# Six output buffers instead of three, no warm matmuls and a new order of sums and scores in the first batch, in an attention plus maxout kernel

## The chip, the cores and the metric

The kernel runs on 1 core of one Trainium2 chip. The metric is the device time of one execution in microseconds (us), the median of several executions. Comparisons are made with the kernel before, timed in the same rounds on the same chip. Ratios use executions in the fast state alone and come with a 95% interval; only one execution on record was counted as slow (354.37 us, of the run with two buffers, over 1.5% above the fastest of that kernel).

Engines: PE is the matmul array, PEld its weight loads, DVE the vector engine, ACT the scalar engine, POOL the general engine that here also issues most loads, SP the engine that issues stores and transposing transfers. A transfer "lands" when all its data has arrived; the landing time is counted from its issue.

## The reference, cut to what matters

```python
# q, k, v: (8, 12, 448, 64); w1, w2, w3, w_out: (768, 768), all float32
scores = scale * np.matmul(q, k.transpose(0, 1, 3, 2))
e = np.exp(scores - m)                       # m is the row maximum
attn = e / (np.sum(e, axis=-1, keepdims=True) + np.exp(-m) + 1e-09)
x = np.matmul(attn, v)                       # then (batch * seq, 768)
h = np.maximum(np.maximum(x @ w1, x @ w2), x @ w3)
out = h @ w_out                              # (3584, 768)
```

## The kernel before

The program is written by hand in the order in which each engine executes it; the tools only add the waits. Heads are taken in groups of 4, so a batch has three groups. For a group, `scores` makes products of k and q in a PSUM buffer and ACT takes the exponential of it; `av` makes the sums over v, and DVE normalises them (`rb`, a reciprocal, `xn`). `x_transpose_pe` brings `xn` into the layout for the second part of the work, `up_piece` makes h (`p_i`), `out_piece` the result (`op_ps`, `o_sb`).

The first batch is cut into an odd part "O" and an even part "E" of the queries, so that PE can begin before all loads are in. "s" in a step is scores, ("v", g, pr) is the sum of group g, head pair pr, part "O".

```python
    out_pool = ctx.enter_context(tc.tile_pool(name="outp", bufs=3))
    ps_s = ctx.enter_context(tc.tile_pool(name="ps_s", bufs=3, space=bass.MemoryType.PSUM))
    ps_b = ctx.enter_context(tc.tile_pool(name="ps_b", bufs=2, space=bass.MemoryType.PSUM))
    # ... cut ...
    def out_piece(bp, t, c, w, queues):
        if c == 0:
            outs[0] = out_pool.tile([128, DM], FP32, tag="o_sb", name="o_sb")
        # ... cut: 6 matmuls into op_ps, DVE copies op_ps to o_sb, two stores on SP ...

    def add_out(b):            # output tiles of a batch: 3, 4, 3, 4, ...
        for t in range(0, 3) if b % 2 == 0 else range(3, 7):
            # ... two pieces of 384 columns each ...

    # ... cut; the first batch, where the change is: ...
    attend("O", 2, S01, S23, S46)
    x_transpose_pe(0, "O")
    warm(2)                    # two matmuls on zeros, result unused
    attend("O", 2, ("v", 1, 0), ("v", 1, 1), ("v", 2, 0))
    attend("E", 0, S01)
    x_transpose_pe(1, "O")
    attend("E", 0, ("v", 2, 1), S23)
    x_transpose_pe(2, "O")
    add_up(0, NE, NO, [(i, f) for i in range(2) for f in (0, 2, 4)])
    fill(STEP)                 # first p_i piece
    attend("E", 0, S46)
    # ... cut; a little later: ...
    load_v(4)
    load_qk(5)
    load_weight(3)             # the output weight, issued by POOL
    # ... cut; later still, POOL copies half blocks of q: shift_q(4, nc.gpsimd)
```

Scores and sums take turns in the three `ps_s` buffers: each waits until ACT or DVE has emptied the one of three tiles ago.

The softmax here doesn't subtract the row's maximum and nothing guards it: scores larger than these inputs give would overflow.

## Time and profile before

| | before |
|---|---|
| time, median of 4 executions | 341.54 us (341.29 to 341.90) |
| time of the execution that was profiled | 342.59 us, span 340.8 us |
| PE / DVE / ACT / POOL busy | 97% / 55% / 44% / 43% |
| share of PE in the chain of waits | 93% |

(The span runs from the first to the last instruction and is about 1.75 us shorter than the time.)

The page of the profile of before, its busy times and the head of its chain:

```profile
PE 330.3 (97%) x4174; PEld 199.6 (59%) x4174; DVE 188.4 (55%) x410; ACT 151.2 (44%) x181; POOL 146.7 (43%) x260
...
PE 93%; ACT 2%; DVE 2%; issue 1%; ACTq 0%
```

PE bounds the kernel; the only thing to win is time in which PE stands still, or work on PE that need not be done. The timeline of PE of before, where the order will change (start, duration, engine, line, operation, out<-in, count; in brackets how long the engine was idle before, and what ended it):

```profile
16.03 1.03 PE L300 MATMUL stp<-QT,KT 64*64 64x192 f16 x24 [0.27 <-DVE QT L186]
17.37 0.28 PE L300 MATMUL stp<-QT,KT 64*64 64x192 f16 x4 [0.30 <-ACT e L320]
17.57 0.40 PE L400 MATMUL xtp<-ident,xn 128*128 128x128 f16 x4
17.81 0.59 PE L171 MATMUL warm<-wz 128*128 128x512 f16 x2
18.33 0.26 PE L340 MATMUL avp<-vt,e 64*64 64x65 f16 x8
...
22.02 0.28 PE L400 MATMUL xtp<-ident,xn 128*128 128x128 f16 x2
22.68 0.28 PE L400 MATMUL xtp<-ident,xn 128*128 128x128 f16 x2 [0.37 <-DVE xn L373]
22.80 1.43 PE L440 MATMUL p_i<-xT,w 128*128 128x192 f16 x12
24.16 0.52 PE L300 MATMUL stp<-QT,KT 64*64 64x256 f16 x12
24.62 1.16 PE L440 MATMUL p_i<-xT,w 128*128 128x192 f16 x12
```

Three things are seen: the warm matmuls at 17.81, a wait for the normalised sum at 22.68, and 12 `p_i` matmuls that take 1.43 us where the next 12 take 1.16, so that a further 0.27 us of waiting (for the copy of the transpose) hides in them. From 67 us on there is one single wait of PE, in the second batch. The timeline of PE there, then of DVE, then the landing times of the two stores issued at 110.0 and 110.5 us:

```profile
114.39 3.09 PE L464 MATMUL op_ps<-w,hT 128*128 128x384 f16 x18
...
118.04 0.93 PE L357 MATMUL avp<-vx,e 128*128 128x65 f16 x24
119.72 3.56 PE L440 MATMUL p_i<-xT,w 128*128 128x448 f16 x18 [0.76 <-DVE o_sb L471]
```

```profile
115.63 0.55 DVE L471 TENSOR_SCALAR o_sb<-op_ps 128x384 f32<-128x384 f32 x1
119.11 1.02 DVE L471 TENSOR_SCALAR o_sb<-op_ps 128x384 f32<-128x384 f32 x2 [2.92 <-PE avp L357]
```

```profile
DMA to landing us min/median/max: 8.1/8.2/8.2
```

The matmuls of the fourth output tile of this batch were done by 117.5 us, but DVE copied them at 119.11. With three buffers that tile reuses the buffer of the first, whose stores landed only 8 us after their issue, the later one at 118.6 us. The wait was for a store.

### The profile page before, as it was taken

What the parts mean: (1) busy time and instruction counts of PE and PEld (TensorE: products, weight loads), DVE (VectorE), ACT (ScalarE), POOL (GpSimd) and SP (SyncE); (2) the same over time, 40 slices, a digit from 0 to 9 for tenths busy, and PEclk for the clock granted to TensorE, in tenths of its full rate; (3) what the DMA queues carried; (4) which work ended last, traced back from release to release, by engine and by line L of the source; (5) the groups of instructions that cost most, each with busy time, mean ns of one, the idle gap of its engine ahead of it and who ended that gap; (6) DMA issues with size and microseconds to landing.
All of it is one profiled execution on the core that took longest, in us unless ns stands there. A gap on an engine that the chain in (4) does not pass through costs nothing.

```text
span 340.8 us, 9819 instructions
## 1 busy us (share of the span) xinstructions
PE 330.3 (97%) x4174; PEld 199.6 (59%) x4174; DVE 188.4 (55%) x410; ACT 151.2 (44%) x181; POOL 146.7 (43%) x260
## 2 busy tenths in 40 slices
PE   7899999999999999999999999999999999999994
PEld 4668787855555645555655655565545655565552
DVE  4556675565545365546456556556556556465552
ACT  3858855654554535463544454463544454200000
POOL 8596578971937072925267070946252000000000
PEclk9999999999999999999999999999999999999999
DMA  8999999699996999999986999999960440133006
GB/s 145 190 191 206 203 205 197 115 170 212 134 164 60 178 213 110 156 138 185 157 119 90 190 199 116 155 127 194 167 115 10 119 123 3 31 78 95 0 19 167
DMA packets 84813, 46.42 MB, mean 136 GB/s; under 512 B 53281, under 2 KB 81313, under 8 KB 84769
## 3 DMA queue, kind: packets, MB, share of 16 engines
q0 software_dynamic: 29120, 21.80, 48.6%
q1 hardware_dynamic: 55264, 23.60, 36.7%
q8 instruction: 32, 0.52, 0.6%
q10 hardware_dynamic: 384, 0.39, 0.4%
q14 instruction: 13, 0.10, 0.1%
HBM read 44.04 MB, written 11.01 MB: 162 GB/s over the span
## 4 chain that ended last, share of the span: by engine, by line
PE 93%; ACT 2%; DVE 2%; issue 1%; ACTq 0%
PE p_i L440 48%; PE op_ps L464 16%; PE avp L357 12%; PE stp L300 12%; PE avp L340 2%; ACT e L320 2%; PE warm L171 1%; PE trT L225 1%; ACT QT L184 1%; DVE QT L186 1%; PE trT L209 1%; DVE xn L373 1%; PE xtp L413 0%; PE xtp L400 0%; DVE xT L406 0%
## 5 line engine op out<-in xcount | busy, mean ns | idle before, releaser
L320 ACT ACTIVATE e<-stp 128x896 f16<-128x896 f32 (+4 forms) x171 | 144.3, 905 | 138.2 <-PE stp L300 138.0
L440 PE MATMUL p_i<-xT,w 128*128 128x448 f16 (+2 forms) x972 | 173.4, 332 | 1.1 <-DVE o_sb L471 0.8
L440 PEld LDWEIGHTS <-w 128*128 128x128 f16 x972 | 90.0, 98 | 69.0 <-issue 6.6
L245 POOL COPY QT<-QT 64x384 f16<-64x384 f16 (+1 forms) x84 | 46.9, 559 | 95.4 <-DMA QT<-ld_q 65.0
L451 DVE TENSOR_TENSOR hT<-hT,p_i 128x448 f16<-128x448 f16 (+2 forms) x96 | 59.7, 621 | 43.0 <-PE p_i L440 42.8
L464 PE MATMUL op_ps<-w,hT 128*128 128x384 f16 (+2 forms) x342 | 58.1, 323 | 0.0
L300 PE MATMUL stp<-QT,KT 64*64 64x448 f16 (+2 forms) x756 | 48.4, 339 | 2.3 <-ACT e L320 0.9
L464 PEld LDWEIGHTS <-hT 128*128 128x128 f16 x342 | 32.1, 98 | 23.0 <-issue 2.0
L471 DVE TENSOR_SCALAR o_sb<-op_ps 128x384 f32<-128x384 f32 (+2 forms) x57 | 31.2, 549 | 25.8 <-PE op_ps L464 22.7
L357 PE MATMUL avp<-vx,e 128*128 128x65 f16 x1152 | 45.4, 193 | 0.0
L449 DVE CAST hT<-p_i 128x448 f16<-128x448 f32 (+2 forms) x48 | 30.0, 625 | 24.3 <-PE p_i L440 24.2
L357 PEld LDWEIGHTS <-e 128*128 128x128 f16 x1152 | 38.8, 97 | 2.3
L373 DVE TENSOR_TENSOR xn<-avp,rb 128x512 f16<-128x512 f32 (+1 forms) x54 | 34.1, 632 | 1.9
L300 PEld LDWEIGHTS <-KT 64*64 64x64 f16 x756 | 16.0, 105 | 27.0 <-issue 24.2
L367 DVE TENSOR_SCALAR rb<-avp 128x8 f32<-128x8 f32 (+1 forms) x54 | 8.9, 165 | 39.4 <-PE avp L357 39.2
L383 POOL COPY vx<-ld_v 128x768 f16<-128x768 f16 x21 | 17.2, 820 | 8.3 <-issue 4.7
L340 PEld LDWEIGHTS <-e 64*64 64x64 f16 x768 | 14.7, 107 | 8.0 <-issue 1.2
L102 POOL DMA_DIRECT2D ld_q<-in_q_dram x24 | 17.2, 718 | 2.1 <-DMA w<-in_moe_w_dram 1.1
L102 POOL DMA_DIRECT2D ld_k<-in_k_dram x24 | 17.2, 718 | 1.9 <-DMA w<-in_moe_w_out_dram 1.0
L115 POOL DMA_DIRECT2D ld_v<-in_v_dram x24 | 15.1, 631 | 2.6 <-DMA w<-in_moe_w_dram 1.4
L340 PE MATMUL avp<-vt,e 64*64 64x65 f16 x768 | 15.4, 192 | 0.5 <-ACT e L320 0.4
L112 POOL DMA_DIRECT2D ld_v<-in_v_dram x24 | 15.2, 633 | 1.2 <-DMA w<-in_moe_w_dram 1.2
(43 smaller groups left out, 88.2 us busy)
## 6 DMA issues: line engine op xcount, KB each, us to landing
out_dram<-o_sb SPq DMA_DIRECT2D x54, 192.0 KB, 3.2
ld_v<-in_v_dram POOLq DMA_DIRECT2D x48, 128.0 KB, 4.8
ld_k<-in_k_dram POOLq DMA_DIRECT2D x23, 224.0 KB, 6.2
ld_q<-in_q_dram POOLq DMA_DIRECT2D x23, 224.0 KB, 7.0
w<-in_moe_w_dram POOLq DMA_DIRECT2D x9, 384.0 KB, 9.5
w<-in_moe_w_out_dram POOLq DMA_DIRECT2D x3, 384.0 KB, 8.5
xT<-xn SPq DMA_TRANSPOSE x18, 4.3
QT<-ld_q SPq DMA_TRANSPOSE x17, 5.1
```

Source lines behind the costliest of these rows:

```text
L102: nc.gpsimd.dma_start(out=tiles[nm][:, 1 : NP * T + 1].rearrange("x (r t) d -> x r (t d)", r=NP)[:, p0:p1], in_=src[:, p0:p1],)
L245: eng.tensor_copy(out=t[d0 : d0 + HP, o * 128 : (o + n) * 128], in_=t[s0 : s0 + HP, a * 128 : (a + n) * 128],)
L300: nc.tensor.matmul(out=stp[half * HP : half * HP + HP, par, j * qn : (j + 1) * qn], lhsT=k_block(i, pr, h2, x[half]), rhs=q_cols(i, pr, h2 ...
L320: nc.scalar.activation(out=dst, in_=src, func=AF.Exp, scale=scale)
L340: nc.tensor.matmul(out=ps[half * HP : half * HP + HP, hh, j * D1 : (j + 1) * D1], lhsT=eF[hh * HP : hh * HP + HP, o : o + HP], rhs=vt[hh * ...
L357: nc.tensor.matmul(out=ps[:, hh, j * D1 : (j + 1) * D1], lhsT=eF[:, o : o + 128], rhs=vx[:, 2 * pr + hh, (x[0]), 0:D1], start=False, stop= ...
L373: nc.vector.tensor_tensor(out=xn[i][:, pr, ws[0] : ws[0] + nw].rearrange("p j h d -> p h j d"), in0=acc[:, :, :, 0:D], in1=rb[:, :, 0:nw]. ...
L440: nc.tensor.matmul(out=p_i[:, j * qn : (j + 1) * qn], lhsT=w_sb[i][:, dc, ts(fc, 128)], rhs=xT[b][:, dc, q0 : q0 + qn], start=(dc == 0), s ...
L449: nc.vector.tensor_copy(out=dst, in_=src)
L451: nc.vector.tensor_tensor(out=dst, in0=dst, in1=src, op=ALU.max)
L464: nc.tensor.matmul(out=op_ps[:, 0:w], lhsT=hT[bp][:, fc, ts(t, 128)], rhs=wout_sb[:, fc, c : c + w], start=(fc == 0), stop=(fc == NFC - 1),)
L471: nc.vector.tensor_scalar(out=o_sb[:, c : c + w], in0=op_ps[:, 0:w], scalar1=1.0 / LAMBDA, scalar2=None, op0=ALU.mult,)
```

## The change

The intent: no output tile waits for an old store; the two sums of group 2 stand next to each other, with the first scores of part E moved ahead of them, so that DVE gets the last normalisation earlier; the warm matmuls go.

```diff
-    out_pool = ctx.enter_context(tc.tile_pool(name="outp", bufs=3))
+    out_pool = ctx.enter_context(tc.tile_pool(name="outp", bufs=6))
 # ... cut ...
     x_transpose_pe(0, "O")
-    warm(2)
-    attend("O", 2, ("v", 1, 0), ("v", 1, 1), ("v", 2, 0))
+    attend("O", 2, ("v", 1, 0))
     attend("E", 0, S01)
+    attend("O", 2, ("v", 1, 1), ("v", 2, 0), ("v", 2, 1))
     x_transpose_pe(1, "O")
-    attend("E", 0, ("v", 2, 1), S23)
+    attend("E", 0, S23)
     x_transpose_pe(2, "O")
```

## The prediction

> **What bounds the kernel.** TensorE. The page of the profile shows PE busy 330.3 of 340.8 us (97%), clock 1.0; the chain of waits is 93% PE; DVE (55%), ACT (44%) and POOL (43%) mostly wait for PE. Only idle time of PE can be won. (The Trainium skill, "Trainium Kernel Development and Optimization", Best Practices, distrusts matmul busy time as a measure; I use it only to find idle spots, which the timeline confirms.)
>
> **What the change does.** Order differs in one place on PE and DVE; ACT, POOL and SP keep theirs.
>
> 1. *Six output buffers.* In the timeline from 67 us on PE stands still in one place: at 119.72 us p_i waits 0.76 us for DVE's o_sb. DVE had been idle 2.92 us before that copy (the releaser named, an avp matmul, was long done: it was something else). It is the fourth output tile of batch 1, so with three buffers it reuses the first, whose stores were issued at 110.0 and 110.5 us and took 8.2 and 8.1 us to land (median of all stores 3.2): until about 118.6; copy at 119.11. Loads of k and q beside it took 9 us too; that all issuers share the same DMA engines, as the skill says ("DMA: Bandwidth & Descriptors", Issuing engines are not separate DMA queues), fits. With six buffers the copy runs at about 117 us and PE saves 0.76 us. Elsewhere, the last stage included, copies follow PE at 0.42 us: nothing to win.
>
> 2. *Reordering, 17.6 to 24.2 us.* The two warm matmuls (17.81, 0.43 us of issue) go. The sum behind them needs a buffer whose exp ends at 18.02; with 0.06 us from exp to PE it starts at about 18.1 instead of 18.33: 0.2 us won, the rest of the warm time becomes a wait. The E scores behind it need the next exp (ends 18.72), just met. Today the chain then runs rb 0.17, reciprocal 0.19, xn 0.44, transposes 0.30, xT copy 0.37, with PE waiting 0.37 us for xn at 22.68 and about 0.3 us for xT, p_i resuming at 23.41. With the second sum of group 2 ahead of group 1's transpose, DVE's four normalisations (about 0.85 us each) stand nearly back to back and set the pace: last xn done at about 22.17 instead of 22.63, p_i resumes at about 22.96. Gain 0.45 us in all, warm share included. The third chunk of the first weight (issued 12.3, 9.9 us to landing) is in by then, barely.
>
> Later waits are relative to PE; the second weight (in at about 30.7, used at 31.7) leaves 0.5 us, so the gain should survive.
>
> **Predicted time.** 341.7 - 0.76 - 0.45 = 340.5; I say 340.6, since the slow landing may be shorter in unprofiled runs. Range 339.7 to 341.5. Faster by over 2%: 0.5%; within 2%: 99%; slower: 0.5%.
>
> **What would show it.** Right: no PE wait near 118 us, o_sb there about 0.4 us behind its matmul; p_i resuming near 23.0; the scores now at 24.16 at 23.7; then a constant shift of 0.45, later 1.2 us. Wrong, part 1: another wait takes its place (earlier stores colliding with the transposing transfers). Wrong, part 2: first sum still at 18.3, or p_i held by the weight load.
>
> **What would make it wrong.** A store wait that is rarer or larger without the profiler; buffers released later than I computed, so that the second sums wait for ACT; gains given back to ACT waits between 24 and 41 us.

## The result, and the profile after

| | before | after |
|---|---|---|
| time, median of 4 executions each | 341.54 us (341.29 to 341.90) | 341.12 us (340.78 to 341.43) |
| ratio | | 0.9987, interval 0.9969 to 1.0004 |
| profiled execution, time | 342.59 us | 341.03 us |
| profiled execution, span | 340.8 us | 339.3 us |

A ratio is the mean time of one kernel's runs over that of the other's of the same rounds, so not quite the ratio of the medians quoted. The interval here includes 1: the timed runs alone do not show the gain, and the argument below rests on traces. (The prediction starts from 341.7 us because only three of the four executions of before had been timed then.)

The profiles differ by 1.5 us, the medians by 0.42 us. The two numbers cannot both be the worth of the change. The page of after shows the same kind of kernel:

```profile
PE 329.4 (97%) x4172; PEld 198.9 (59%) x4172; DVE 189.3 (56%) x410; ACT 151.1 (45%) x181; POOL 146.6 (43%) x260
...
PE 91%; ACT 2%; DVE 2%; DMA 2%; issue 1%; POOL 1%; POOLq 0%; ACTq 0%
```

The timeline of PE of after, at the place of the new order:

```profile
15.94 1.03 PE L300 MATMUL stp<-QT,KT 64*64 64x192 f16 x24 [0.27 <-DVE QT L186]
17.27 0.28 PE L300 MATMUL stp<-QT,KT 64*64 64x192 f16 x4 [0.30 <-ACT e L320]
17.48 0.40 PE L400 MATMUL xtp<-ident,xn 128*128 128x128 f16 x4
17.97 0.26 PE L340 MATMUL avp<-vt,e 64*64 64x65 f16 x8
...
21.64 0.29 PE L400 MATMUL xtp<-ident,xn 128*128 128x128 f16 x2
22.21 0.28 PE L400 MATMUL xtp<-ident,xn 128*128 128x128 f16 x2 [0.28 <-DVE xn L373]
22.47 1.29 PE L440 MATMUL p_i<-xT,w 128*128 128x192 f16 x12
23.69 0.52 PE L300 MATMUL stp<-QT,KT 64*64 64x256 f16 x12
24.14 1.16 PE L440 MATMUL p_i<-xT,w 128*128 128x192 f16 x12
```

The first sum follows the transpose sooner, the wait for `xn` fell from 0.37 to 0.28 us, and the `p_i` matmuls take 1.29 instead of 1.43 us. The timeline of PE of after in the second batch, then of DVE:

```profile
113.92 3.09 PE L464 MATMUL op_ps<-w,hT 128*128 128x384 f16 x18
...
118.33 3.56 PE L440 MATMUL p_i<-xT,w 128*128 128x448 f16 x18
```

```profile
115.16 0.55 DVE L471 TENSOR_SCALAR o_sb<-op_ps 128x384 f32<-128x384 f32 x1
116.06 0.56 DVE L471 TENSOR_SCALAR o_sb<-op_ps 128x384 f32<-128x384 f32 x1 [0.36 <-PE op_ps L464]
117.04 0.56 DVE L471 TENSOR_SCALAR o_sb<-op_ps 128x384 f32<-128x384 f32 x1 [0.42 <-PE op_ps L464]
```

The copies follow their matmuls, and PE does not wait: the wait of 0.76 us is gone.

**How the traces are compared from here on.** The start of the program is not the same from one execution to the next: the first scores of group 2 (the 24 matmuls at 16.03 above) start anywhere from 15.55 to 16.22 us in the profiles, in an order of instructions that is the same up to there. One source is at the very start. The Trainium skill ("TensorE: Matmul & The Clock Gate", What's actually happening) says that the number of slow first matmuls varies from run to run. It does here: the seven transposes at 4.9 us took 0.94 us in before and 0.57 in e1. Another source was a wait of 0.36 us for a load of q at 9.93 us in e1. So I measure from these scores on: to the second `p_i` piece (24.62 above), and to the `p_i` after the fourth output tile (119.72 above). For the kernels with three or more output buffers that differ in nothing but the parts of the change, that gives (us):

| kernel | output buffers | order | warm | to 2nd p_i | to p_i of second batch | span |
|---|---|---|---|---|---|---|
| before | 3 | old | yes | 8.59 | 103.69 | 340.8 |
| before, again | 3 | old | yes | 8.59 | 102.76 | 339.8 |
| buffers alone | 6 | old | yes | 8.58 | 102.76 | 339.7 |
| no warm | 3 | old | no | 8.35 | 102.53 | 341.5 |
| no warm, 6 buffers | 6 | old | no | 8.35 | 102.53 | 339.5 |
| new order, warm kept | 3 | new | yes | 8.41 | 102.59 | 339.2 |
| order alone | 3 | new | no | 8.20 | 102.38 | 339.2 |
| after | 6 | new | no | 8.20 | 102.39 | 339.3 |
| after, again | 6 | new | no | 8.21 | 102.39 | 339.2 |
| new order, 4 buffers | 4 | new | no | 8.21 | 102.38 | 339.6 |

Kernels with the same order and the same warm matmuls agree within 0.01 us over 100 us, with one exception: the first profile of before, 0.93 us longer than all others of its kind.

### The profile page after: what moved, and what is told of

It is laid out like the page before. It is cut to its first block, busy times and chain, and to the rows that moved or that the text cites. A ratio compares the mean times of both kernels' runs of the same rounds, so it can differ in the third digit from the quotient of the medians.

```text
span 339.3 us, 9812 instructions
## 1 busy us (share of the span) xinstructions
PE 329.4 (97%) x4172; PEld 198.9 (59%) x4172; DVE 189.3 (56%) x410; ACT 151.1 (45%) x181; POOL 146.6 (43%) x260
## 4 chain that ended last, share of the span: by engine, by line
PE 91%; ACT 2%; DVE 2%; DMA 2%; issue 1%; POOL 1%; POOLq 0%; ACTq 0%
PE p_i L440 48%; PE op_ps L464 16%; PE avp L357 11%; PE stp L300 11%; PE avp L340 2%; ACT e L320 2%; DMA ld_q<-in_q_dram 2%; DVE xn L373 1%; PE trT L225 1%; DVE QT L186 1%; PE xtp L413 0%; ACT QT L184 0%; POOL ld_k L102 0%; PE xtp L400 0%; DVE rb L370 0%
## 5 line engine op out<-in xcount | busy, mean ns | idle before, releaser
L471 DVE TENSOR_SCALAR o_sb<-op_ps 128x384 f32<-128x384 f32 (+2 forms) x57 | 31.3, 549 | 23.7 <-PE op_ps L464 23.5
L449 DVE CAST hT<-p_i 128x448 f16<-128x448 f32 (+2 forms) x48 | 30.0, 625 | 23.7 <-PE p_i L440 23.6
```

The source lines that it names most:

```text
L449: nc.vector.tensor_copy(out=dst, in_=src)
L471: nc.vector.tensor_scalar(out=o_sb[:, c : c + w], in0=op_ps[:, 0:w], scalar1=1.0 / LAMBDA, scalar2=None, op0=ALU.mult,)
```

## The experiments

Theory A: the wait for the store is typical of the kernel before; the buffers are worth 0.76 us. Theory B: the profiled execution of before was an untypical one; the buffers are worth nothing in most executions, and what the medians show is the order alone.

### e1_before_again: the kernel before, once more

Edit: none.

> The kernel before, unchanged, profiled and timed a second time. Theory A (the store wait is typical of it): the span is again about 340.8 us and the 0.76 us wait of the p_i matmuls near 119.7 us is there again. Theory B (the profiled execution of before, 342.59 us against a median of 341.5, was an untypical one and the store wait is rare or smaller otherwise): span about 339.8 us, wait near 119.7 us absent or under 0.3 us. Ratio to before 1.000 in both; its interval is the noise of this method.

Measured: median 341.55 us, ratio to before 0.9992 (0.9976 to 1.0009), span 339.8 us. DVE and PE at the place of the wait, and the landing times of the same two stores:

```profile
115.70 0.55 DVE L471 TENSOR_SCALAR o_sb<-op_ps 128x384 f32<-128x384 f32 x1
117.50 1.02 DVE L471 TENSOR_SCALAR o_sb<-op_ps 128x384 f32<-128x384 f32 x2 [1.25 <-DMA out_dram<-o_sb]
```

```profile
118.10 0.93 PE L357 MATMUL avp<-vx,e 128*128 128x65 f16 x24
118.87 3.57 PE L440 MATMUL p_i<-xT,w 128*128 128x448 f16 x18
```

```profile
DMA to landing us min/median/max: 6.0/6.2/6.5
```

DVE waits for the store here too, and this time the profile names it. But the store took 6.5 us at most instead of 8.2, DVE copied at 117.50, and PE had not run out of its two `ps_b` buffers. DVE waits at this copy in all five profiles with three buffers (1.21 to 2.92 us); PE feels it only when the landing is late enough. From the first profile: the copy started at 119.11 and cost 0.93 us, so a copy by about 118.2, or a landing within about 7.2 us, would have cost nothing (an estimate from these numbers, with the 0.48 us that passed between the landing at 118.63 and the copy). The second profile is as theory B expected: span 339.8 us, no wait of PE.

### e2_buffers_alone: six buffers, old order

```diff
-name="outp", bufs=3
+name="outp", bufs=6
```

> Six output buffers, old order. Theory A: 0.7 to 0.8 us faster than before (ratio 0.9978), no PE wait near 119 us. Theory B: no more than 0.2 us faster (ratio 0.9994 or more), since the wait it removes is mostly not there.

Measured: median 341.77 us, ratio 1.0001 (0.9982 to 1.0020). In the trace the way to the second batch is 102.76 us, exactly as in before again. The timed runs show no gain of the buffers alone. Their interval still allows about 0.6 us either way, but the 0.76 us of theory A (ratio 0.9978) lies just outside it. One of the six executions took 342.82 us with six buffers, where a store would have to take some 20 us to be waited for (an estimate from the pauses given in e13), so late stores are very likely not the only cause of slow executions; that execution was not profiled.

### e3_order_alone: new order, three buffers

```diff
 (the change, with bufs=3)
```

> New order, three output buffers. Both theories expect the scores after the first p_i piece about 0.4 us earlier (23.7 instead of 24.2). Theory A: 0.4 us faster than before, and the store wait of 0.7 us is still there near 119 us. Theory B: 0.4 us faster, as fast as the whole change, store wait absent or different from profile to profile.

Measured: median 341.25 us against 341.68, ratio 0.9982 (0.9965 to 0.9999). In the trace 8.20 and 102.38 us, the same as the whole change, and no PE wait in the second batch (DVE waited 1.34 us before the copy at 117.04, which fits the store of the first tile that landed about 116.5; that is within the slack). In these traces the order and the missing warm matmuls are the whole gain when no store is late.

### e4_no_warm: only the warm matmuls taken out

```diff
     x_transpose_pe(0, "O")
-    warm(2)
     attend("O", 2, ("v", 1, 0), ("v", 1, 1), ("v", 2, 0))
```

> Old order and three buffers, only the two warm matmuls taken out. The first sum of group 1 starts at about 18.1 instead of 18.3 us; if the chain of DVE normalisations passes this on, 0.2 us faster in the trace at 24 us (scores at 23.95). If the warm matmuls are needed to keep the array's clock up, the matmuls after 18 us become longer and the time does not fall.

Measured: in the trace 8.35 instead of 8.59 us, so 0.24 us of the 0.43 us in which PE issues the two warm matmuls is won, and kept to the second batch (102.53). The matmuls that follow do not become longer. But the time was no better, median 341.80 us, from 340.78 to 343.63, with two of six executions over 343 us. The profiled one (343.23 us) shows why, in PE and DVE of the fourth batch:

```profile
194.87 0.93 PE L357 MATMUL avp<-vx,e 128*128 128x65 f16 x24
197.66 1.67 PE L440 MATMUL p_i<-xT,w 128*128 128x448 f16 x8 [1.86 <-DVE o_sb L471]
```

```profile
192.47 0.55 DVE L471 TENSOR_SCALAR o_sb<-op_ps 128x384 f32<-128x384 f32 x1
197.05 1.02 DVE L471 TENSOR_SCALAR o_sb<-op_ps 128x384 f32<-128x384 f32 x2 [4.03 <-DMA out_dram<-o_sb]
```

The same wait, at another fourth tile, now worth 1.86 us: the slower of the first tile's two stores took 8.8 us to land. So two of the five profiles with three buffers show a stall of PE by a store (before 0.76, this one 1.86 us), and none of the eight with four or six.

### e5_order_with_warm: new order, warm matmuls kept, three buffers

```diff
 (the change, with bufs=3, and)
     x_transpose_pe(0, "O")
+    warm(2)
     attend("O", 2, ("v", 1, 0))
```

> New order with the two warm matmuls kept, three buffers: the order without the warm matmuls gone. If the start of the first sum carries through (the chain is one of PE), the scores after the first p_i piece stand about 0.2 us later than in the new order alone (23.9 against 23.69), so the order alone is worth 0.1 to 0.2 us of the 0.4. If DVE's normalisations set the pace whatever the start, it is as fast as the new order alone.

Measured: median 341.26 us, ratio 0.9990 (0.9978 to 1.0002). In the trace 8.41 us, 0.21 more than the new order alone: the first of the two expectations. With e4 the two parts can be told apart: the warm matmuls are worth 0.24 us in the old order and 0.21 in the new, the order 0.18 with them and 0.15 without; together 0.39 at the second `p_i` piece and 0.37 in the second batch.

### e6_2buf: two output buffers, to force the wait

```diff
-name="outp", bufs=3
+name="outp", bufs=2
```

> The kernel before with two output buffers, to make the wait for a store happen in every execution. Three buffers wait only when the store of three tiles ago takes over about 8 us (slack of about 2 us between the DVE wait and PE standing still); with two, the third tile of each half has about 2 to 4 us less. Expected: several PE waits released by o_sb at the halves that start near 108, 150, 187, 227, 265 us, 1 to 5 us each, and 6 to 16 us slower. If the wait near 119 us of the first profile had nothing to do with the stores, it is no slower than 1 us.

Measured: median 352.27 us over all four executions, 351.96 over the three fast ones; ratio of the fast ones 1.0276 (1.0236 to 1.0316), about 10 us slower. The waits in its profile (who waited for whom, us in total, times, longest), and one of them in the timeline of PE:

```profile
DVE o_sb L471 <- DMA out_dram<-o_sb: 16.0, 6, 5.3
...
PE op_ps L464 <- DVE o_sb L471: 6.7, 5, 3.1
...
PE p_i L440 <- DVE o_sb L471: 2.3, 3, 1.0
```

```profile
117.57 1.14 PE L464 MATMUL op_ps<-w,hT 128*128 128x384 f16 x6 [2.43 <-DVE o_sb L471]
```

PE waits 9.0 us in eight places, all through DVE, which waits for stores. This shows the mechanism by experiment, and that three buffers stood just at the edge: two cost about 10 us, three stalled PE in two of five profiles.

### e9_no_warm_6buf: no warm matmuls, six buffers

```diff
 (e4, and)
-name="outp", bufs=3
+name="outp", bufs=6
```

> Old order without the warm matmuls, six buffers. The same kernel with three buffers had two of six executions over 343 us and a 1.86 us wait for a store in its profile. If those slow executions were store waits: none over 342.2 us here and a median of about 341.4 us. If they came from anything else, such as a colder array, slow executions stay.

Measured: median 341.26 us (341.14 to 341.58), ratio 0.9992 (0.9979 to 1.0005), none of five executions over 341.6 us; the trace again 102.53 us, with no wait of PE for a store. As expected if the slow executions of e4 were late stores. Only one of those two was profiled, and these ran on another chip, so for the other this is likely and not shown.

### e13_order_4buf: new order, four buffers

```diff
 (the change, with bufs=4)
```

> New order with four output buffers. A half has at most four tiles, so four should do what six do: DVE's o_sb copies of the fourth tile near 117 and 195 us follow their matmuls by 0.42 us and do not wait for a store (with three buffers they did, by about 0.9 us or more). Same time as the whole change within 0.2 us.

Measured: median 341.32 us, ratio 0.9989 (0.9976 to 1.0001). (A half is the run of three or four output tiles that `add_out` puts in one place.) The copies of the fourth tiles start 0.36 us after DVE fell idle, released by their matmuls, at 116.10 and 193.28 us, as with six buffers; with three they started at 117.04 and 194.16 in the profile of the order alone. In this trace four are enough, because a half has at most four tiles and the halves are at least 20 us apart (the copies of one end at 308 us in before, those of the next begin at 328.9).

### e8_split_scores: part of the next scores ahead of the second transpose

PE still waits 0.28 us for `xn` at 22.21 in after. This fills the gap with work that is ready.

```diff
 (the change, and)
-    attend("E", 0, S23)
+    attend("E", 0, S23, S46[:2])
     x_transpose_pe(2, "O")
     add_up(0, NE, NO, [(i, f) for i in range(2) for f in (0, 2, 4)])
     fill(STEP)
-    attend("E", 0, S46)
+    attend("E", 0, ("s", (6,)))
```

> The changed kernel with the first two score units of the next step moved ahead of the second transpose, into the 0.28 us in which PE waits for xn at 22.2 us. Expected about 0.3 us earlier from 24 us on than the changed kernel, 0.3 us faster (340.8 us against 341.1), if ACT is not made late by it.

Measured: median 341.77 us (340.96 to 342.95), ratio 1.0005 (0.9989 to 1.0021). The expectation failed. To the second `p_i` piece it is 7.99 us, 0.21 less than after; to the second batch 103.08, 0.69 more. PE and POOL of this run show where it was lost:

```profile
39.80 3.02 PE L440 MATMUL p_i<-xT,w 128*128 128x256 f16 x24
42.99 0.38 PE L300 MATMUL stp<-QT,KT 64*64 64x448 f16 x2 [0.18 <-POOL QT L245]
43.66 0.57 PE L300 MATMUL stp<-QT,KT 64*64 64x448 f16 x6 [0.29 <-POOL QT L245]
```

```profile
39.73 1.41 POOL L126 DMA_DIRECT2D w<-in_moe_w_out_dram  x2 [1.19 <-DMA w<-in_moe_w_dram]
...
42.44 2.52 POOL L245 COPY QT<-QT 64x384 f16<-64x384 f16 x4
```

The scores of group 4 need copies of QT that POOL makes. Their input was ready at 37.6 us, but POOL first issues the three loads of the output weight (and two of v), and stood idle 1.07 and 1.19 us before two of them, for an earlier weight load to land as the profile puts it. In after the copies started at 40.92 us, in this run at 42.44, while PE came early. Much of that is chance: counted from the first scores, the copies start 24.4 to 26.0 us later in the other profiles with these issues in front of them, and 26.9 in this one. So they were at least 0.9 us later than in any other, more than the 0.2 us by which PE was early.

### e10_split_wout_late and e11_wout_late: the output weight's loads behind those copies

```diff
 (e8 for e10, the change for e11, and)
     load_v(4)
     load_qk(5)
-    load_weight(3)
 # ... cut ...
             shift_q(i + 1, nc.gpsimd)
         if first:
+            load_weight(3)
             load_qk(i + 3)
```

> The split of the scores (the run that won 0.2 us at 24 us and lost it at 43 us to POOL's copies of QT) with the loads of the output weight issued after those copies instead of before. If the loss was POOL standing behind its own weight-load issues, the QT copies start near 38.5 us instead of 42.4, no PE wait for POOL near 43 us, and the time is 0.2 to 0.3 us under the whole change of the same rounds (about 340.8 us). If the loss had another cause, it stays near 341.7 us.

> The whole change with only the output weight's loads moved behind the QT copies. In the profile of the whole change those copies were just in time (40.92 against scores at 43.34), so nothing is won in a typical execution: within 0.2 us of the whole change; its slowest executions may be gone. Output weight still in by 67 us, so no new wait at the first output tile.

Measured: e10 median 341.39 us, ratio 0.9983 (0.9970 to 0.9996); e11 341.31 us, 0.9988 (0.9976 to 1.0000). POOL and PE of e10:

```profile
38.91 2.38 POOL L245 COPY QT<-QT 64x384 f16<-64x384 f16 x4
```

```profile
40.46 3.02 PE L440 MATMUL p_i<-xT,w 128*128 128x256 f16 x24
43.41 0.57 PE L300 MATMUL stp<-QT,KT 64*64 64x448 f16 x8
```

The wait for POOL is gone and the 0.22 us stay: e10 needs 102.17 us to the second batch, e11 102.39, after 102.39. From the start of this `p_i` to the end of the eight scores e8 takes 4.43 us and e10 3.52, so the whole 0.91 us between the two was lost here. The copies of e10 start 22.7 us after the first scores, earlier than in any profile with the issues in front. So the loss of e8 was POOL behind its own issues, in an execution with slow loads; each of the two kernels was profiled once. The timed runs do not resolve the 0.2 us: the median of e10 is not below that of e11, and its profile began with the latest start of all (16.22 us). On the traces from the first scores on it is the shortest version; on the clock it is a tie with after.

### e12_after_again: the whole change once more

Edit: none beyond the change.

> The whole change again, on the chip of this call. 0.4 us faster than before (ratio 0.9988, as the new order alone), not 1.2 us: the store wait that six buffers remove is absent from most executions of before.

Measured: median 341.36 us against 341.75, ratio 0.9987 (0.9974 to 1.0000): 0.39 us of the medians, as expected. Its trace repeats after within 0.01 us.

## Why the prediction was right or wrong, point by point

- **PE bounds the kernel, and the change stays within 2%.** Right. 341.12 us lies in the predicted range of 339.7 to 341.5 us. That is partly luck: the range was wide enough to hold although the larger of the two gains, 0.76 of 1.21 us, is mostly absent from the timed executions.
- **"With six buffers the copy runs at about 117 us and PE saves 0.76 us."** The mechanism was right: the copies ran at 116.06 and 117.04 us, the wait was one for a store (named so in e1, forced in e6), and it cost even 0.93 us in that profile. One step towards it was wrong: the `avp` matmuls that the profile names had not been "long done", they ended 0.14 us before the copy, and only e1 rules them out. The size was wrong for the metric. In the term "341.7 - 0.76 - 0.45", the 0.76 came from an execution of 342.59 us and was taken off a median of executions in which it mostly does not occur: six buffers alone gave a ratio of 1.0001. The prediction allowed 0.1 us for "the slow landing may be shorter in unprofiled runs"; it should have allowed nearly all of it. The prediction did name the risk ("a store wait that is rarer"), and the hint was in the data: the profiled execution was 0.69 us slower than the slowest timed one, about as much as the wait.
- **"Gain 0.45 us in all, warm share included."** Right in sign and path, a little too large: 0.39 us at the second `p_i`, 0.37 in the second batch. The warm share was put at 0.2 us and measured 0.21 to 0.24. The rest was put at 0.25 and measured 0.15 to 0.18. The last `xn` was done at 22.15 us, which is 22.24 on the clock of before (the first scores of after start 0.09 us earlier), against 22.17 in the prediction: that is the missing 0.07. Which step of the estimate lost it is not shown. The scores now stand between the first two sums, so DVE waits 0.25 us between the first two normalisations, which were to stand "nearly back to back"; but the four took 3.40 us with that wait, just what four of "about 0.85 us" come to. Because of the earlier start it is partly luck that the next scores stand at 23.69 where 23.7 was predicted.
- **"The gain should survive."** It did, to 0.02 us (0.39 and 0.37), through the ACT waits of 24 to 41 us that I had named as a danger. The danger was elsewhere: e8 shows that POOL's copies of QT for group 4 stand close behind, and that a further 0.2 us would have met them in an execution with slow loads. I had not looked at POOL's queue.
- **The sum.** Predicted gain 1.1 us, measured 0.42 in the first comparison and 0.39 in the second; the difference is nearly all the store term. Between the two executions that were profiled first, both terms are there: to the `p_i` of the second batch 103.69 and 102.39 us, 1.30 apart, of which 0.93 is the store.

What stays open is how often a store is late enough to stall PE with three buffers. Two of five profiles show it, which is too few for a rate. Stalls as large as the first may be rarer than that: of the 37 timed executions of before only one (343.39 us) was slower than the profiled one (342.59). Smaller stalls the timed executions cannot tell, since kernels with six buffers also had executions 1 us above their median (342.82 and 342.95 us) whose traces I do not have.

## What to carry to other kernels

Before a wait found in a profile is credited to a change, compare the time of the profiled execution with the timed ones: a wait for a DMA can belong to that one execution, and a second profile of the same kernel costs one run. When effects are far below the noise of whole runs, measure between two fixed instructions of the trace; here that repeated to 0.01 us where the whole times of one kernel with three or more buffers scattered by 0.4 to 2.9. A buffer count that is just enough is an insurance question and not one of the median: count the tiles that can be in flight between two pauses (four here), and give that many.

## What the Trainium skill lacked or had wrong

- "DMA: Bandwidth & Descriptors", Issuing engines are not separate DMA queues, says that transfers of all issuers interleave on the same engines. The traces fit: while the two stores of SP took 8.1 to 8.2 us in before, the loads of k and q that POOL had issued about 2 us before them took 9.1 and 9.4 (medians 6.2 and 7.0). They add a spread that the page does not give: stores of the same size, at the same place of the program, took 6.0 to 6.5 us to land in one profile of the kernel before and 8.1 to 8.2 in the other, against medians of 3.5 and 3.2 over all stores of these profiles; in e4 one took 8.8.
- "Perfetto Trace Analysis", Identifying Dependency Chains, says that an instruction that waits on several engines may get separate semaphore instructions ahead of it. It does not say how to tell which of several waits ended last. Here the 2.92 us before the copy at 119.11 us were put down to the `avp` matmuls, which ended at 118.97; the same wait was named as the store in the next profile. What told them apart was that next profile, in which the copy ran at 117.50, before these matmuls began; the landing of the store at 118.6 us in the first one fits.
- No page that I found says that POOL's issue of a load can itself wait for an earlier load to land, so that computing of POOL behind it waits too: in e8 POOL stood idle 1.07 and 1.19 us before issues of the output weight, and copies whose input had been ready at 37.6 us started at 42.44. With these issues moved behind the copies they started at 38.91 (e10).
